# Gated linear attention and a top-1 router: attention outputs built head-columns-first in column tiles, with one scan over all head pairs

## The chip, the cores and the metric

The kernel runs on one core of a Trainium2 chip. Five engines work from queues of their own: TensorE (PE in the rows; PEld is its weight loads), VectorE (DVE), ScalarE (ACT), GpSimd (POOL) and SyncE (SP, which issues most transfers). The metric is device time in microseconds for one execution, median of the runs.

## What is computed

Attention with a gated state, then a router that sends each token to one expert of eight:

```python
batch, n_heads, seq, head_dim = (4, 8, 768, 48)
for t in range(S):
    state = alpha[:, :, t, :, None] * state + np.einsum('bhd,bhe->bhde', k[:, :, t], v[:, :, t])
    y[:, :, t] = np.einsum('bhd,bhde->bhe', q[:, :, t], state)
x = np.ascontiguousarray(attn_out.transpose(0, 2, 1, 3)).reshape(B * S, H * D)   # 3072 x 384
xn = x / (np.linalg.norm(x, axis=-1, keepdims=True) + 1e-06)
logits = xn @ en.T / tau
expert_idx = np.argmax(logits, axis=1)
...
    h = np.maximum(x[mask] @ w1[e], 0.0)
    out[mask] = gate_w[mask, None] * (h @ w2[e])
```

All is float32. A matmul that multiplies float32 leaves two records in the trace (two weight loads and two passes); a transpose leaves one.

## The kernel before

Three parts follow each other. **Attention** (lines 100 to 340) goes over 24 chunks of 128 tokens, six for each batch. **Routing** (lines 343 to 429) sorts the tokens by expert. **The expert blocks** (lines 432 to 518) gather 128 tokens at a time, run two matmuls with the expert's weights and scatter the rows. Only attention is touched by the change.

In attention the eight heads of 48 columns are padded to 64 and taken in four pairs, so that a pair fills 128 partitions after a transpose. For chunk s, `load` fetches alpha, q, k and v (`at`, `qt`, `kt`, `vt`, 192 KB each). `decays` transposes alpha, k and q on PE (`pa`, `pk`, `pq`, four transposes each), and VectorE runs two scans for each of the four pairs: `a`, the running product from the chunk's start, and `r`, the one from its end. Then `kr` = k times `r`, and `qs` = q times `a` over the chunk's whole decay. `scores` multiplies `kr` and `qs` head by head, 64 partitions at a time (`sc`), and masks them (`sm`). `update` turns `kr` back (`pkb`, copied to `kb`), multiplies it with v for the new state (`pd`) and adds the decayed old one. `rows` builds the outputs with tokens on partitions (`py`): for each pair one matmul with the decayed state and two with the masked scores. `logits` transposes those rows (`px`, copied to `xT`) and multiplies by the expert embeddings (`pl`). After the sixth chunk of a batch `choose` picks experts: a string of 13 small VectorE operations, with an activation table change on ScalarE.

The loop (lines 329 to 340) is a software pipeline: step s runs `decays(s)`, `scores` and `update` of s-1, `rows` of s-2 and `logits` of s-3. A scheduler at build time keeps nearly this order on each engine, and each engine runs its list in order. Transposed tiles share three PSUM buffers (`ps_tr`: `pa`, `pk`, `pq`, `pkb`, `px`), `pd`, `py` and `pl` three others (`ps_mm`), and `sc` has one buffer of two banks.

## Time and profile before

| | us |
|---|---|
| median of 3 runs (594.1 to 600.29) | 600.13 |
| the profiled execution | 600.23 |
| its span, first to last instruction | 598.5 |

| engine | busy, us | share of the span |
|---|---|---|
| PE | 512.8 | 86% |
| PEld | 430.7 | 72% |
| DVE | 197.9 | 33% |
| ACT | 96.1 | 16% |
| POOL | 85.1 | 14% |

Attention takes the span up to about 226 us, routing up to about 270 us, the expert blocks the rest. In the rows, a start is in microseconds from the span's first instruction. Records of PE overlap their neighbours, so that the rate of matmuls is read from the difference of two starts, not from a duration.

### The profile page before, as it was taken

What the parts mean: (1) busy time and instruction counts of PE and PEld (TensorE: products, weight loads), DVE (VectorE), ACT (ScalarE), POOL (GpSimd) and SP (SyncE); (2) the same over time, 40 slices, a digit from 0 to 9 for tenths busy, and PEclk for the clock granted to TensorE, in tenths of its full rate; (3) what the DMA queues carried; (4) which work ended last, traced back from release to release, by engine and by line L of the source; (5) the groups of instructions that cost most, each with busy time, mean ns of one, the idle gap of its engine ahead of it and who ended that gap; (6) DMA issues with size and microseconds to landing.
All of it is one profiled execution on the core that took longest, in us unless ns stands there. A gap on an engine that the chain in (4) does not pass through costs nothing.

```text
span 598.5 us, 9056 instructions
## 1 busy us (share of the span) xinstructions
PE 512.8 (86%) x3536; PEld 430.7 (72%) x3536; DVE 197.9 (33%) x602; ACT 96.1 (16%) x194; POOL 85.1 (14%) x141
## 2 busy tenths in 40 slices
PE   5799889979988993729999999999999999991993
PEld 4688778869877982618877877877877877860881
DVE  6867766784676444610001011011011011000100
ACT  2222232241232223000110100100100100100010
POOL 2110021011001000131102122122122121002010
PEclk9999999996998796558999999999999999996897
DMA  9968875673650000094084774914814939286000
GB/s 155 168 124 148 143 126 92 133 133 67 124 102 13 21 34 14 1 361 166 26 288 170 243 251 157 321 51 162 316 41 160 317 100 305 96 284 196 9 28 16
DMA packets 130011, 84.72 MB, mean 142 GB/s; under 512 B 101879, under 2 KB 121379, under 8 KB 129952
## 3 DMA queue, kind: packets, MB, share of 16 engines
q1 hardware_dynamic: 126336, 73.93, 47.2%
q0 software_dynamic: 3456, 10.03, 4.7%
q8 instruction: 31, 0.51, 0.3%
q14 instruction: 28, 0.23, 0.1%
q10 hardware_dynamic: 160, 0.01, 0.0%
HBM read 109.13 MB, written 10.03 MB: 199 GB/s over the span
## 4 chain that ended last, share of the span: by engine, by line
PE 70%; DVE 13%; issue 9%; ACT 3%; DMA 2%; another core or an unknown queue 1%; POOL 1%; POOLq 0%; ACTq 0%
PE ph L484 22%; PE pyo L494 21%; PE py L293 7%; PE py L284 4%; DVE a L202 4%; PE pd L244 4%; DVE r L203 4%; PE pl L317 3%; DMA xg<-x_rows,gidx 2%; PE pa L175 2%; PE inv L399 2%; PE sc L268 2%; DVE kr L215 2%; PE px L310 1%
## 5 line engine op out<-in xcount | busy, mean ns | idle before, releaser
L484 PEld LDWEIGHTS ph<-xgT,w 128*128 128x128 f32 x1296 | 151.4, 196 | 11.9 <-DVE xgT L477 7.9
L484 PE MATMUL ph<-xgT,w 128*128 128x128 f32 x1296 | 153.4, 279 | 5.5 <-DVE xgT L477 5.5
L494 PE MATMUL pyo<-w,hT 128*128 128x384 f32 x432 | 143.8, 486 | 0.0
L494 PEld LDWEIGHTS pyo<-w,hT 128*128 128x128 f32 x432 | 80.0, 190 | 50.1
L498 DVE TENSOR_SCALAR y<-pyo,bgate 128x384 f32<-128x384 f32 x27 | 16.7, 618 | 263.7 <-PE pyo L494 263.7
L490 ACT ACTIVATE hT<-ph 128x512 f32<-128x512 f32 x54 | 32.2, 597 | 320.9 <-PE ph L484 320.9
L293 PE MATMUL py<-vt,sm 128*128 128x48 f32 x384 | 56.4, 277 | 0.0
L499 POOL DMA_INDIRECT out_dram<-y,sidx x27 | 27.0, 1001 | 187.6 <-DVE y L498 185.2
L293 PEld LDWEIGHTS py<-vt,sm 128*128 128x128 f32 x384 | 53.0, 203 | 0.0
L202 DVE TENSOR_TENSOR_SCAN a<-pa,zeros 128x128 f32<-128x128 f32 x96 | 38.8, 404 | 22.0 <-PE pa L175 22.0
L465 POOL DMA_INDIRECT xg<-x_rows,gidx x27 | 27.9, 1032 | 105.8 <-PE pxg L475 77.9
L475 PE MATMUL pxg<-ident,xg 128*128 128x128 f32 x81 | 14.9, 320 | 27.2 <-DMA xg<-x_rows,gidx 18.6
L203 DVE TENSOR_TENSOR_SCAN r<-pa,zeros 128x127 f32<-128x127 f32 x96 | 38.0, 396 | 0.0
L284 PE MATMUL py<-decayed,qs 128*128 128x96 f32 x160 | 35.6, 306 | 0.0
L475 PEld LDWEIGHTS pxg<-ident,xg 128*128 128x128 f32 x81 | 10.9, 162 | 33.3 <-issue 30.4
L272 DVE TENSOR_TENSOR sm<-sc,causal 128x512 f32<-128x512 f32 x48 | 31.1, 678 | 1.9 <-PE sc L268 1.9
L268 PE MATMUL sc<-qs,kr 64*128 64x128 f32 x384 | 30.6, 302 | 0.0
L268 PEld LDWEIGHTS sc<-qs,kr 64*128 64x128 f32 x384 | 25.6, 203 | 4.7 <-issue 3.8
L477 DVE COPY xgT<-pxg 128x384 f32<-128x384 f32 x27 | 14.1, 550 | 42.0 <-PE pxg L475 23.5
L244 PE MATMUL pd<-vt,kb 128*128 128x96 f32 x160 | 23.3, 290 | 4.7 <-ACT kb L241 4.7
L219 DVE SCALAR_TENSOR_TENSOR qs<-pq,rend,a 128x128 f32<-128x128 f32 x96 | 26.9, 340 | 0.0
L239 PE MATMUL pkb<-ident,kr 128*128 128x128 f32 x80 | 13.5, 292 | 15.5 <-DVE r L203 15.5
(117 smaller groups left out, 391.0 us busy)
## 6 DMA issues: line engine op xcount, KB each, us to landing
w<-in_moe_w_dram SPq DMA_DIRECT2D x54, 1536.0 KB
at<-in_alpha_dram SPq DMA_DIRECT2D x24, 192.0 KB
qt<-in_q_dram SPq DMA_DIRECT2D x24, 192.0 KB
kt<-in_k_dram SPq DMA_DIRECT2D x24, 192.0 KB
vt<-in_v_dram SPq DMA_DIRECT2D x24, 192.0 KB
x_rows<-x SPq DMA_DIRECT2D x24, 192.0 KB
xg<-x_rows,gidx POOLq DMA_INDIRECT x27, 5.3
out_dram<-y,sidx POOLq DMA_INDIRECT x27, 5.8
```

Source lines behind the costliest of these rows:

```text
L202: nc.vector.tensor_tensor_scan(a[:, p], pa[:, p], zeros, 1.0, ALU.mult, ALU.add)
L203: nc.vector.tensor_tensor_scan(r[:, p, P - 2 :: -1], pa[:, p, P - 1 : 0 : -1], zeros[:, 0 : P - 1], 1.0, ALU.mult, ALU.add,)
L244: nc.tensor.matmul(pd[:, 2 * p * D : 2 * (p + 1) * D], lhsT=kb[:, p], rhs=vt[:, 2 * p : 2 * p + 2].rearrange("p h d -> p (h d)"), start=Tr ...
L268: nc.tensor.matmul(sc[:, hh, p], lhsT=kr[sl, p], rhs=qs[sl, p], start=True, stop=True)
L272: nc.vector.tensor_tensor(sm[:, hh], sc[:, hh], causal.to_broadcast([P, NP, P]), ALU.mult)
L284: nc.tensor.matmul(py[:, 2 * p * D : 2 * (p + 1) * D], lhsT=qs[:, p], rhs=decayed[:, p].rearrange("p j e -> p (j e)"), start=not opened, s ...
L293: nc.tensor.matmul(py[:, h * D : (h + 1) * D], lhsT=sm[:, hh, p], rhs=vt[:, h], start=not opened, stop=True, skip_group_check=True,)
L465: nc.gpsimd.indirect_dma_start(out=xg, out_offset=None, in_=x_rows, in_offset=bass.IndirectOffsetOnAxis(ap=gidx[:, j : j + 1], axis=0), bo ...
L484: nc.tensor.matmul(ph[:, f], lhsT=w1_t[:, i, (f0 + f) * P : (f0 + f + 1) * P], rhs=xgT[:, i], start=(i == 0), stop=(i == KT - 1),)
L490: nc.scalar.activation(hT[:, f0 : f0 + 4], ph, AF.Relu)
L494: nc.tensor.matmul(py, lhsT=hT[:, f], rhs=w2_t[:, f], start=(f == 0), stop=(f == FT - 1))
L499: ins = nc.gpsimd.indirect_dma_start(out=out, out_offset=bass.IndirectOffsetOnAxis(ap=sidx[:, j : j + 1], axis=0), in_=y, in_offset=None, ...
```

## The change

- **Outputs.** `py` now has head columns on partitions and tokens in the free dimension. `mix_states` (four matmuls of 128 x 128, with the decayed state as weights) and `mix_chunk` (eight matmuls with 64 columns of weights, each head writing its own half of the partitions: a column tile) replace the twelve matmuls of `rows`. The result is copied to `yT`.
- **Rows and logits.** Four matmuls `px`, with `yT` as weights and a constant `sel` as the moving operand (96 columns that pick the tokens' rows, 8 that are the expert embeddings), give both. They replace the three transposes `px`, the copy `xT` and three matmuls `pl`. The four logit parts are added by one VectorE reduction.
- **State.** `pd` is computed head by head in column tiles (eight matmuls, 64 weight columns and 64 moving columns) in place of four matmuls of pairs. The state is 128 x 256, and its decayed copy `dec` is block diagonal, written by two GpSimd operations on 64 partitions each; the sum is two VectorE operations.
- **Scans.** One scan of 511 and one of 512 elements replace eight of 127 and 128. They are restarted at the pair borders by a zero in alpha (a GpSimd memset of the first token's row in `at`) and a start value in the second operand (`inr`, `ini`). The lost first alpha comes from a separate small load `a0`, turned at the start into `al0`. `qs` is one operation for four.
- **Order.** Step s now begins with `keys_back(s-1)`, `mix_states(s-2)` and `rows(s-3)`, ahead of `decays(s)`; `mix_chunk(s-2)` comes last. k is loaded ahead of q.

The core of the diff:

```diff
         def load(s):
...
             nc.sync.dma_start(out=at_s[i][:, :, 0:D], in_=a_r[b, c])
+            nc.gpsimd.memset(at_s[i][0:1], 0.0)
+            nc.sync.dma_start(out=kt_s[i][:, :, 0:D], in_=k_r[b, c])
             nc.sync.dma_start(out=qt_s[i][:, :, 0:D], in_=q_r[b, c])
...
+            a0 = work.tile([NS, H, DP], FP32, name="a0", bufs=1)
+            nc.gpsimd.memset(a0[:, :, D:DP], 1.0)
+            for b in range(B):
+                nc.scalar.dma_start(
+                    out=a0[b * NCH : (b + 1) * NCH, :, 0:D], in_=a_r[b, :, 0]
+                )
...
-            for p in range(NP):
-                nc.vector.tensor_tensor_scan(a[:, p], pa[:, p], zeros, 1.0, ALU.mult, ALU.add)
-                nc.vector.tensor_tensor_scan(
-                    r[:, p, P - 2 :: -1], pa[:, p, P - 1 : 0 : -1], zeros[:, 0 : P - 1],
-                    1.0, ALU.mult, ALU.add,
-                )
+            nc.vector.tensor_tensor_scan(
+                r[:, L - 2 :: -1], pa[:, L - 1 : 0 : -1], inr[:, L - 2 :: -1],
+                1.0, ALU.mult, ALU.add,
+            )
...
+            nc.vector.tensor_tensor_scan(a, pa, ini, 0.0, ALU.mult, ALU.add)
...
+            for p in range(NP):
+                for hh in range(2):
+                    h = 2 * p + hh
+                    nc.tensor.matmul(
+                        pd[DP * hh : DP * hh + DP, p],
+                        lhsT=kb[:, h * DP : (h + 1) * DP],
+                        rhs=vt[:, h],
+                        start=True, stop=True,
+                    )
...
+        def mix_states(s):
+            d = st[s]
+            d["py"] = py = ps_mm.tile([P, NP, P], FP32, tag="mm", name="py")
+            dec = d.get("dec")
+            if dec is not None:
+                for p in range(NP):
+                    nc.tensor.matmul(
+                        py[:, p], lhsT=dec[:, p].rearrange("p j e -> p (j e)"),
+                        rhs=d["qs"][:, p],
+                        start=(p == 0), stop=False, skip_group_check=True,
+                    )
+
+        def mix_chunk(s):
+
+            d = st[s]
+            py, sm, vt = d["py"], d["sm"], vt_s[s % NBV]
+            for p in range(NP):
+                for hh in range(2):
+                    nc.tensor.matmul(
+                        py[DP * hh : DP * hh + DP, p],
+                        lhsT=vt[:, 2 * p + hh], rhs=sm[:, hh, p],
+                        start=("dec" not in d and p == 0), stop=True, skip_group_check=True,
+                    )
+            d["yT"] = yT = work.tile([P, NP, P], FP32, name="yT")
+            nc.scalar.copy(yT, py)
...
+            yT = st[s]["yT"]
+            px = ps_mm.tile([P, NP, 2 * D + E], FP32, tag="mm", name="px")
+            for p in range(NP):
+                nc.tensor.matmul(px[:, p], lhsT=yT[:, p], rhs=sel[:, p], start=True, stop=True)
+            x = work.tile([P, NP, 2 * D], FP32, name="x", bufs=3)
+            nc.scalar.copy(x, px[:, :, 0 : 2 * D])
+            nc.vector.tensor_reduce(
+                lg[:, s].unsqueeze(2), px[:, :, 2 * D :].rearrange("t p e -> t e p"),
+                axis=AX.X, op=ALU.add,
+            )
...
             if s + 2 < NS:
                 load(s + 2)
+            if 0 <= s - 1 < NS:
+                keys_back(s - 1)
+            if 0 <= s - 2 < NS:
+                mix_states(s - 2)
+            if 0 <= s - 3 < NS:
+                rows(s - 3)
             if s < NS:
                 decays(s)
             if 0 <= s - 1 < NS:
+                decay_state(s - 1)
                 scores(s - 1)
                 update(s - 1)
             if 0 <= s - 2 < NS:
-                rows(s - 2)
-            if 0 <= s - 3 < NS:
-                logits(s - 3)
+                mix_chunk(s - 2)
```

**PE, one full chunk in the second batch's pipeline.** The order's counts are matmuls as written; each that is no transpose leaves two records. Before:

```order
L175 MATMUL pa<-ident,at_124 128x128 x4
L175 MATMUL pk<-ident,kt_132 128x128 x4
L175 MATMUL pq<-ident,qt_128 128x128 x4
L268 MATMUL sc<-qs,kr 128x128 x8
L239 MATMUL pkb<-ident,kr 128x128 x4
L310 MATMUL px<-ident,x 128x128 x3
L244 MATMUL pd<-vt,kb 128x96 x4
L284 MATMUL py<-decayed,qs 128x96
L293 MATMUL py<-vt,sm 128x48 x2
```

The last two rows stand there four times, and `pl` x3 ends the step. Of the change, from the same transposes on:

```order
L216 MATMUL pa<-ident,at_118 128x128 x4
L216 MATMUL pk<-ident,kt_126 128x128 x4
L216 MATMUL pq<-ident,qt_122 128x128 x4
L326 MATMUL sc<-qs,kr 128x128 x8
L303 MATMUL pd<-vt_129,kb 64x64 x8
L352 MATMUL py<-sm,vt_128 64x128 x8
L275 MATMUL pkb<-ident,kr 128x128 x4
L340 MATMUL py<-qs,dec_168 128x128 x4
L365 MATMUL px<-sel,yT 128x104 x4
```

`pkb` has moved behind the other work of its step, `pd` and `py` work in halves of 64 columns, and `pl` is gone.

**VectorE, one chunk.** (The order calls a scan SCALAR_TENSOR_TENSOR.) Before:

```order
L202 SCALAR_TENSOR_TENSOR a<-pa,zeros 128x128
L203 SCALAR_TENSOR_TENSOR r_149<-pa,zeros 128x127
L202 SCALAR_TENSOR_TENSOR a<-pa,zeros 128x128
L203 SCALAR_TENSOR_TENSOR r_149<-pa,zeros 128x127
L202 SCALAR_TENSOR_TENSOR a<-pa,zeros 128x128
L203 SCALAR_TENSOR_TENSOR r_149<-pa,zeros 128x127
L202 SCALAR_TENSOR_TENSOR a<-pa,zeros 128x128
L203 SCALAR_TENSOR_TENSOR r_149<-pa,zeros 128x127
L209 RECIPROCAL rend<-a 128x4
L272 TENSOR_TENSOR sm<-sc,causal 128x512
L215 TENSOR_TENSOR kr<-pk,r_149 128x512
L219 SCALAR_TENSOR_TENSOR qs<-pq,rend,a 128x128 x4
```

Of the change:

```order
L368 TENSOR_REDUCE lg<-px 128x8
L246 SCALAR_TENSOR_TENSOR r_152<-pa,inr 128x511
L253 TENSOR_TENSOR kr<-pk,r_152 128x512
L256 RECIPROCAL ini_154<-r_152 128x4
L260 SCALAR_TENSOR_TENSOR a<-pa,ini_154 128x512
L266 TENSOR_TENSOR qs<-pq,a 128x512
L330 TENSOR_TENSOR sm<-sc,causal 128x512 x2
L315 TENSOR_TENSOR state<-pd,dec_166 64x256 x2
```

The logits' reduction now stands ahead of the scans of the next chunk, and `kr` comes between the two scans.

**GpSimd, the third and fourth chunk.** Of the change:

```order
L228 MEMSET at_116 1x512
L263 TENSOR_TENSOR end<-r_151,al_173 128x4
L228 MEMSET at_117 1x512
L287 TENSOR_TENSOR dec_166<-state,end 64x4x64 x2
L263 TENSOR_TENSOR end<-r_152,al_173 128x4
```

Before, `ends` and `decayed` simply took turns there. Now a memset that waits for a later chunk's alpha to land stands ahead of each decayed state.

## Rows read from the trace of the kernel before

**Rows 1.** The page's part 4: shares of the chain that ended last, by engine

```profile
PE 70%; DVE 13%; issue 9%; ACT 3%; DMA 2%; another core or an unknown queue 1%; POOL 1%; POOLq 0%; ACTq 0%
```

**Rows 2.** Stretch, length, busy PE, PEld, DVE, ACT, POOL; clock, DMA share, GB/s

```profile
6.58:52.46 45.88, 39.59 (x328) 34.79 (x328) 34.74 (x104) 8.39 (x19) 5.16 (x10) 1.00 0.97 149
52.46:104.24 51.78, 45.66 (x420) 41.19 (x420) 37.61 (x119) 14.19 (x34) 6.27 (x16) 1.00 0.74 127
104.24:159.94 55.70, 49.97 (x420) 45.89 (x420) 37.71 (x119) 15.47 (x35) 6.27 (x16) 0.91 0.57 107
159.94:225.80 65.86, 59.93 (x498) 55.27 (x498) 39.40 (x123) 17.86 (x42) 6.28 (x16) 0.90 0.23 52
```

**Rows 3.** PE in order of time, 85 to 95 us: start, us, line, records

```profile
85.30 0.51 PE L310 MATMUL px<-ident,x 128*128 128x128 f32 x3
85.64 0.60 PE L175 MATMUL pa<-ident,at 128*128 128x128 f32 x4
...
87.99 1.16 PE L268 MATMUL sc<-qs,kr 64*128 64x128 f32 x16
89.71 0.66 PE L239 MATMUL pkb<-ident,kr 128*128 128x128 f32 x4 [0.56 <-DVE r L203]
90.50 0.55 PE L310 MATMUL px<-ident,x 128*128 128x128 f32 x3
91.04 1.13 PE L244 MATMUL pd<-vt,kb 128*128 128x96 f32 x8
92.01 0.39 PE L284 MATMUL py<-decayed,qs 128*128 128x96 f32 x2
...
94.65 0.80 PE L317 MATMUL pl<-embT,xT 128*128 128x8 f32 x6
95.31 0.31 PE L175 MATMUL pa<-ident,at 128*128 128x128 f32 x1
```

**Rows 4.** PE's weight loads in the same stretch

```profile
87.99 0.97 PEld L268 LDWEIGHTS sc<-qs,kr 64*128 64x128 f32 x16 [0.17 <-issue]
91.04 0.97 PEld L244 LDWEIGHTS pd<-vt,kb 128*128 128x128 f32 x8 [0.23 <-ACT kb L241]
```

**Rows 5.** Groups of VectorE, 52 to 104 us: busy us, mean ns, idle before; L365 later

```profile
L202 DVE TENSOR_TENSOR_SCAN a<-pa,zeros 128x128 f32<-128x128 f32 x24 | 9.7, 404 | 3.6 <-PE pa L175 3.6
L272 DVE TENSOR_TENSOR sm<-sc,causal 128x512 f32<-128x512 f32 x12 | 7.7, 677 | 0.0
L215 DVE TENSOR_TENSOR kr<-pk,r 128x512 f32<-128x512 f32 x6 | 4.1, 689 | 0.1
L255 DVE TENSOR_TENSOR state<-pd,decayed 128x384 f32<-128x384 f32 x4 | 2.2, 546 | 0.0
...
L365 DVE TENSOR_TENSOR_SCAN start<-nb,zeros 128x8 f32<-128x8 f32 x1 | 0.2, 175 | 0.0
```

**Rows 6.** Groups of ScalarE and GpSimd, 52 to 104 us

```profile
L232 POOL TENSOR_TENSOR decayed<-state,ends 128x384 f32<-128x384 f32 x5 | 4.1, 828 | 16.8 <-DVE state L255 13.6 <-ACT state L253 3.3
L301 ACT COPY x<-py 128x384 f32<-128x384 f32 x7 | 3.4, 479 | 22.8 <-PE py L293 22.8
L241 ACT COPY kb<-pkb 128x512 f32<-128x512 f32 x5 | 2.9, 586 | 16.0 <-PE pkb L239 16.0
```

**Rows 7.** Busy time by stretch: two idle spots of PE and what follows each

```profile
130.00:134.00 4.00, 1.63 (x19) 1.20 (x15) 4.00 (x18) 0.83 (x2) 1.32 (x7) 1.00 0.98 177
134.00:144.00 10.00, 10.00 (x53) 9.67 (x53) 3.92 (x13) 1.47 (x4) 0.83 (x1) 0.54 0.25 59
```

**Rows 8.** The span's start in order of time, ScalarE, SyncE and PE

```profile
1.42 0.36 ACTq L127 DMA_DIRECT2D rtau<-in_moe_tau_dram  x1
4.21 0.79 SPq L183 DMA_DIRECT2D at<-in_alpha_dram  x1
6.19 0.45 PE L138 MATMUL pe<-ident,emb 8*128 8x8 f32 x3 [6.19 <-DVE emb L135]
6.58 1.11 PE L175 MATMUL pa<-ident,at 128*128 128x128 f32 x4
```

**Rows 9.** Busy time by stretch while the first chunks load

```profile
15.00:30.00 15.00, 11.49 (x109) 9.93 (x107) 12.88 (x37) 3.33 (x7) 2.07 (x4) 1.00 1.03 168
```

More of the change, by code (lines that the diff above doesn't have):

```diff
@@ L67 @@
     nc.gpsimd.memset(zeros, 0.0)
-    half = consts.tile([P, NP, 2], FP32)
-    nc.gpsimd.memset(half, 0.0)
-    nc.gpsimd.memset(half[0:DP, :, 0:1], 1.0)
-    nc.gpsimd.memset(half[DP:P, :, 1:2], 1.0)
     cols_i = consts.tile([P, P], I32)
@@ L90 @@
     rtau = consts.tile([P, 1], FP32)
-    embT = consts.tile([P, KT, E], FP32)
     gidx = consts.tile([P, NBLK], I32)
@@ L101 @@
         pads = c1.enter_context(tc.tile_pool(name="pads", bufs=1))
-        loads = c1.enter_context(tc.tile_pool(name="loads", bufs=6))
         work = c1.enter_context(tc.tile_pool(name="work", bufs=2))
@@ L111 @@
         kt_s = [pads.tile([P, H, DP], FP32, name=f"kt{i}") for i in range(NBUF)]
+        vt_s = [pads.tile([P, H, DP], FP32, name=f"vt{i}") for i in range(NBV)]
         for i in range(NBUF):
@@ L115, with prepare @@
             nc.vector.memset(kt_s[i][:, :, D:DP], 0.0)
+        for i in range(NBV):
+            nc.vector.memset(vt_s[i][:, :, D:DP], 0.0)
         NR = 3
-        r_s = [pads.tile([P, NP, P], FP32, name=f"r{i}") for i in range(NR)]
+        r_s = [pads.tile([P, NP * P], FP32, name=f"r{i}") for i in range(NR)]
+        ini_s = [pads.tile([P, NP * P], FP32, name=f"ini{i}") for i in range(2)]
+        inr = pads.tile([P, NP * P], FP32, name="inr")
+        nc.gpsimd.memset(inr, 0.0)
         for i in range(NR):
-            nc.vector.memset(r_s[i][:, :, P - 1 : P], 1.0)
+            nc.vector.memset(r_s[i][:, NP * P - 1 :], 1.0)
+        for i in range(2):
+            nc.vector.memset(ini_s[i], 0.0)
+        for p in range(NP - 1):
+            nc.gpsimd.memset(inr[:, p * P + P - 1 : (p + 1) * P], 1.0)
+        ND = 3
+        dec_s = [pads.tile([P, NP, 2, DP], FP32, name=f"dec{i}") for i in range(ND)]
+        for i in range(ND):
+            nc.gpsimd.memset(dec_s[i], 0.0)
         chunk_of = "b h (c p) d -> b c p h d"
         a_r, q_r, k_r, v_r = (t.rearrange(chunk_of, p=P) for t in (alpha, q, k, v))
-        def prepare_experts():
+        sel = pads.tile([P, NP, 2 * D + E], FP32, name="sel")
+        al0 = pads.tile([P, NP, NS], FP32, name="al0")
+        def prepare():
             emb = work.tile([E, DM], FP32, name="emb", bufs=1)
@@ L207, in decays @@
-            end = a[:, :, P - 1 : P]
-            rend = work.tile([P, NP, 1], FP32, name="rend")
-            nc.vector.reciprocal(rend, end)
-            if c > 0:
-                d["ends"] = ends = work.tile([P, NP, 2], FP32, name="ends", bufs=3)
-                nc.gpsimd.tensor_tensor(ends, half, end.to_broadcast([P, NP, 2]), ALU.mult)
+            nc.vector.tensor_tensor_scan(
+                r[:, L - 2 :: -1], pa[:, L - 1 : 0 : -1], inr[:, L - 2 :: -1],
+                1.0, ALU.mult, ALU.add,
+            )
@@ new lines, in keys_back, with decay_state @@
+        def keys_back(s):
+            if s % NCH == NCH - 1:
+                return
+            kr = st[s]["kr"]
+            pkb = ps_tr.tile([P, NP * P], FP32, tag="tr", name="pkb")
+            for p in range(NP):
+                nc.tensor.transpose(pkb[:, p * P : (p + 1) * P], kr[:, p], ident)
+            st[s]["kb"] = kb = work.tile([P, NP * P], FP32, name="kb")
+            nc.scalar.copy(kb, pkb)
+        def decay_state(s):
+            if s % NCH == 0:
+                return
+            d = st[s]
+            dec = d["dec"] = dec_s[s % ND]
+            for hh in range(2):
+                sl = slice(DP * hh, DP * hh + DP)
+                nc.gpsimd.tensor_tensor(
+                    dec[sl, :, hh], carried["state"][sl],
+                    d["end"][sl].to_broadcast([DP, NP, DP]), ALU.mult,
@@ L300, in rows @@
-            d["x"] = x = work.tile([P, DM], FP32, name="x", bufs=3)
-            nc.scalar.copy(x, py[:, 0:DM])
-            nc.sync.dma_start(out=x_rows[s * P : (s + 1) * P], in_=x)
-            x2 = work.tile([P, DM], FP32, name="x2")
-            nc.scalar.activation(x2, x, AF.Square, accum_out=sq[:, s : s + 1])
-        def logits(s):
-            x = st[s]["x"]
-            px = ps_tr.tile([P, 512], FP32, tag="tr", name="px")
-            for j in range(KT):
-                nc.tensor.transpose(
-                    px[:, j * P : (j + 1) * P], x[:, j * P : (j + 1) * P], ident
-                )
-            xT = work.tile([P, KT, P], FP32, name="xT")
-            nc.scalar.copy(xT.rearrange("p j t -> p (j t)"), px[:, 0 : KT * P])
-            pl = ps_mm.tile([P, 512], FP32, tag="mm", name="pl")
-            for j in range(KT):
-                nc.tensor.matmul(
-                    pl[:, 0:E], lhsT=xT[:, j], rhs=embT[:, j],
-                    start=(j == 0), stop=(j == KT - 1),
-                )
-            nc.vector.tensor_copy(lg[:, s], pl[:, 0:E])
+                nc.tensor.matmul(px[:, p], lhsT=yT[:, p], rhs=sel[:, p], start=True, stop=True)
```

130 lines of the change are left out of this document (60 added, 70 removed).

## The prediction

> **What bounds the kernel now.** I read the chain that ended last first: TensorE carries 70% of it and VectorE 13% [rows 1]. Then I split the span into stretches [rows 2]. The first row begins with the first alpha transpose; each of the first three ends where the next batch's begins, and the last ends with attention. In the undisturbed second batch TensorE is busy for 45.66 of 51.78 us, VectorE for 37.61, ScalarE for 14.19, and the transfers take a 0.74 share. So attention is TensorE's, with VectorE close behind. Third I read one chunk of TensorE in order of time, by differences of starts [rows 3]. Three transposes take 85.30 to 85.64, 0.11 us for each record. The eight records of `pd` (96 moving columns) take 0.97, 0.12 each. The 24 of `py` (48 and 96 columns mixed) take 92.01 to 94.65, 0.11 each, and the six of `pl` (8 columns) take 0.66, again 0.11. So up to 128 moving columns a record of the full array costs 0.11 us whatever its width. The exception is `sc`, which works in two halves of 64 rows: its 16 loads take 0.97, 0.06 each, with 0.17 us lost ahead of them [rows 4]. Two half arrays run at once.
>
> A full chunk so has 19 transposes (2.09), `sc` (0.97 + 0.17), `pd` (0.97), `py` (2.64) and `pl` (0.66), 7.50 us. A batch has six, less one `pkb` and `pd` (1.41) in the last chunk and the four state matmuls (0.88) in the first: 42.7 us. The other 9.1 of the 51.78 are waits, 1.5 a chunk. They are seen in [rows 3]: `pkb` waits 0.56 us for a buffer that the scans still read, then two hand-overs through ScalarE.
>
> **The change part by part, on TensorE.** Transposes fall from 19 to 16: 1.76. `mix_states`: 8 records of the full array, 0.88. `px`: 8 records, 0.88. `sc` stays, 1.14. `mix_chunk`: 16 records of 64 weight columns and 128 moving ones. No row shows a column tile. The nearest row is `sc`, the other way to split the array, with as many records and the same 128 columns: I take its 0.97, and 0.17 for one more change of shape. The bounds are 0.97 and 16 x 0.11 = 1.76 if halves take turns. `pd`: 16 records of 64 and 64 columns. The lower bound is half of `sc`'s 0.97, 0.49, the upper also 1.76; I take 0.73, between half and whole of the row that it is nearest to, and 0.17 for going back to the full array. Sum: 1.76 + 0.88 + 0.88 + 1.14 + 1.14 + 0.90 = 6.70 us.
>
> On the change of shape the Trainium skill (TensorEngine Tiling (Array Packing), Key Properties) says that changing the tiling mode drains TensorE. The 0.17 us ahead of `sc` agree [rows 4], and it speaks against this change, which has one such border more per chunk.
>
> **Waits of the new order.** `mix_states` of the next step needs the buffer that `yT`'s copy frees, and `px` needs `yT`. That copy is of the size of `kb`'s, 0.59 us [rows 6], and it can start only when the last record has run out, some 0.2 us behind its issue (the four of `pkb` are issued in 0.44 us and end 0.66 us after the first began [rows 3]). Only `pkb`'s 0.44 lies beside it, with its border: 0.2 us of stall, so 6.9 us a chunk. `pkb` itself has moved behind `sc`, `pd` and `py`, about 4.4 us behind its step's first transpose. The scans that held its buffer then need about 4.1 (next paragraph). That cover is thin: if VectorE is late by 1 us, about 0.7 of it shows in every chunk.
>
> **VectorE.** A scan of 128 takes 404 ns, one of 8 takes 175 [rows 5], 1.9 ns an element. So one of 512 is 404 + 384 x 1.9 = 1.14 us, against four at 404. Bounds: 1.05 (the same less the overlap of neighbours) and 1.62. Per chunk: two scans 2.28, `kr` and `qs` 0.60 each (689 ns less the overlap with the next, about 0.09), `sm` twice 1.2, the reciprocal 0.15 (a small operation: the 8-wide scan takes 0.175), the two halves of the state about 0.35 each (546 ns for 384 elements, now 256), the logits' reduction 0.2: 5.8 us. It stands now at 37.61 / 6 = 6.3. Begun 0.9 us behind the first transpose (the reduction waits for ScalarE's copy of `px`), its first scan, `kr`, reciprocal and second scan end at 0.9 + 1.14 + 0.65 + 0.2 + 1.14 = 4.1. So VectorE has about 1 us to spare in 6.9, except where `choose` adds its 13 operations of about 0.17 us, 2.2 in all: I let 1.5 us of them show per batch.
>
> **ScalarE and GpSimd.** ScalarE trades the copies `xT` for `yT`, 0.59 for 0.48, and has 14.19 of 51.78 us to do: covered. GpSimd has two multiplies on half the partitions for one of 828 ns [rows 6], at most 1.7 us, and the memset behind alpha's load. That load is issued more than one step before it is needed. The loads of one chunk are 0.786 MB, 4.7 us at the 168 GB/s of [rows 9], under 6.9. If that cover went, `dec` would come late and with it `mix_states`, at the price of the load's lateness.
>
> **The start and the end.** Four transfers for `a0` come ahead of ScalarE's first table load, about 0.4 us of issue each as for `rtau` [rows 8], 1.6 in all. GpSimd's memset for the padded embedding now stands behind the landing of the second alpha, issued at 4.21 and behind 4.7 us of the first chunk's loads, so near 8 us. The embedding's transposes, which start at 6.19, move to about 9, with four more behind them. The first alpha transpose moves from 6.58 to about 9.8: +3.2. (Bounds +2 and +5.) The last chunk's `yT` and `px` lengthen the drain by 0.6 + 0.9, and its two part steps are shorter by 0.5 each: +0.4.
>
> **Sum.** A batch: 6 x 6.9 less `pkb`, `pd` and `mix_states` once (0.44 + 0.73 + 0.88), plus 1.5: 40.9 against 51.78, a gain of 10.9. The first batch took 45.88 with the filling [rows 2]; I estimate its first three steps, which lack the later stages and go by VectorE's 4.1 us of scans, at 5.0, 5.5 and 6.0, and the rest at 3 x 6.9: 37.2, less 3.2 for the late start: gain 5.5. Batches three and four carry a stretch at the lower clock each. Where TensorE had been busy for only 1.63 of 4 us, the next 10 us ran at 0.54, that is almost wholly at 1.2 GHz in place of 2.4 [rows 7]; batch three is 3.9 longer than batch two for it [rows 2]. `choose` stays, so I leave these as they are. Gain 5.5 + 3 x 10.9 - 0.4 = 37.8. Routing and the expert blocks are untouched. The profiled execution has 600.2 (span 598.5), as has the median, 600.13: **562 us**.
>
> **Rivals.** (A) *VectorE sets the pace.* If a long scan costs four short ones (1.62) and each of five dependent operations adds 0.1 us, VectorE needs 5.8 + 1.0 + 0.5 = 7.3 us a chunk, 6 x 7.3 + 2.2 = 46.0 a batch, a gain of 5.8: 562 + 3 x 5.1 = 577. For it: VectorE is now at 73% of the batch and would be near 90%. Against: [rows 5] show the slope.
>
> (B) *Column tiles take turns.* Then the change does not do what it says. `mix_chunk` alone: +0.79 in 24 chunks, 581. `pd` too: another 1.03 in 20, 602, no change. The gain of 37.8 over 24 chunks is 1.6, so it is used up when the 32 half records cost 1.70 + 1.6 = 3.3 us, 0.10 each, which is about what a full one costs. For it: both halves of `py` write the same PSUM bank, those of `sc` write two. Against: `sc`'s halves run at once at the same width.
>
> (C) *Slower: loads stop hiding.* If in column tiles a weight load can't run beside a matmul, a record costs half a load and a full matmul, about 0.055 + 0.11 = 0.165; 32 of them are 5.3 us, +3.6 in some 22 chunks: 641. It decides from 0.10 each, as in (B). Against: eight loads and eight matmuls of `pd` fit into the same 0.97 us [rows 3, 4]. The Trainium skill (TensorE: Matmul & The Clock Gate, Part 3: Packing small matmuls — row/col tiling) would make this likelier: it has loads overlap with matmuls under way only where the row group differs, and column tiles share theirs. The trace disagrees: `pd` uses all rows in every record, and its loads are hidden all the same.
>
> **How the numbers follow.** My forecast gets 0.68, (A) 0.14, (B) 0.12, (C) 0.06. Around 562: `pd`'s bounds are 0.24 x 20 = 5 us on either side; both low-clock stretches gone would give 8, two more would cost 8; the start is worth 2. That is 549 to 577 for the likeliest case, and to take in (A) and the first half of (B) the range goes to 588. The measurement can tell about 1%, 6 us, from no change. Forecast and (A) are faster, of (B) a half is; the other half is the same, (C) slower, with a hundredth of the forecast's for a gain that something unseen takes back: faster 0.87, same 0.07, slower 0.06.
>
> **What would show it.** Right: records of `mix_chunk` in pairs, 16 in about 1 us; `pd`'s 16 in 0.5 to 1; batches of about 41 us; VectorE above 85% busy in them; the first alpha transpose near 10 us. Wrong: half records 0.11 apart (B) or more (C); TensorE waiting for VectorE ahead of `pkb` in each chunk (A); GpSimd's memset waiting long for alpha; more stretches at the low clock, since what idles TensorE there is `choose`, and that is unchanged.

## The result and the profile after

The changed kernel takes 542.65 us (median; 542.2 to 543.53) beside 600.21 for the kernel before on the same chip: ratio 0.9065, 95% interval 0.9006 to 0.9124. It is faster by 57.6 us, where 37.8 were forecast, and lies 6 us below the range: the sign and the place of the gain were right, the size was not. The profiled execution has 542.78, its span 541.0.

The chain that ended last, by engine (the page's part 4), answers to [rows 1]:

```profile
PE 58%; DVE 23%; issue 12%; DMA 2%; another core or an unknown queue 1%; POOL 1%; ACT 1%; POOLq 0%; DVEq 0%; ACTq 0%
```

VectorE carries 23% of it, up from 13. The stretches, cut as in [rows 2] (from the first alpha transpose; each to the next batch's; the last to the start of the last `x` copy), with the same columns:

```profile
10.33:45.17 34.84, 34.42 (x382) 31.12 (x382) 31.42 (x50) 8.54 (x18) 10.12 (x24) 1.00 0.86 177
45.17:82.21 37.04, 36.07 (x454) 32.97 (x453) 35.53 (x70) 14.63 (x32) 11.83 (x28) 1.00 0.82 176
82.21:120.83 38.62, 36.14 (x454) 32.96 (x453) 36.81 (x71) 15.91 (x33) 11.30 (x27) 1.00 0.71 152
120.83:168.40 47.57, 42.62 (x526) 38.47 (x524) 40.78 (x79) 19.19 (x41) 10.52 (x25) 1.00 0.29 72
```

| us | before [rows 2] | after | change | forecast |
|---|---|---|---|---|
| up to the first alpha transpose | 6.58 | 10.33 | +3.75 | +3.2 |
| batch 1 | 45.88 | 34.84 | -11.04 | -8.7 |
| batch 2 | 51.78 | 37.04 | -14.74 | -10.9 |
| batch 3 | 55.70 | 38.62 | -17.08 | -10.9 |
| batch 4, to its last `x` | 65.86 | 47.57 | -18.29 | -10.5 |
| the rest of the span | 372.7 | 372.6 | -0.1 | 0 |

All of the gain lies in the attention part. Two things stand out. TensorE's granted clock is 1.00 in all four stretches, where batches 3 and 4 had 0.91 and 0.90. And VectorE is busy for 35.53 of 37.04 us in batch 2 (96%), as near to the batch's length as TensorE with 36.07.

One chunk of TensorE in order of time (start, us, line, records), which answers to [rows 3]:

```profile
33.07 0.60 PE L216 MATMUL pa<-ident,at 128*128 128x128 f32 x4
33.50 0.60 PE L216 MATMUL pk<-ident,kt 128*128 128x128 f32 x4
33.94 0.60 PE L216 MATMUL pq<-ident,qt 128*128 128x128 f32 x4
34.47 1.16 PE L326 MATMUL sc<-qs,kr 64*128 64x128 f32 x16
35.56 0.69 PE L303 MATMUL pd<-vt,kb 128*64 128x64 f32 x16
36.08 1.05 PE L352 MATMUL py<-sm,vt 128*64 128x128 f32 x16
37.05 0.66 PE L275 MATMUL pkb<-ident,kr 128*128 128x128 f32 x4
37.55 1.06 PE L340 MATMUL py<-qs,dec 128*128 128x128 f32 x8
38.44 1.04 PE L365 MATMUL px<-sel,yT 128*128 128x104 f32 x8
39.31 0.60 PE L216 MATMUL pa<-ident,at 128*128 128x128 f32 x4
```

By differences of starts the chunk takes 39.31 - 33.07 = 6.24 us, with no wait in it. `mix_chunk` (line 352) issues its 16 records in 0.97, `pd` its 16 in 0.52. The trace has the single records too: within `sc` and `mix_chunk` two half records start together every 0.11 us, as long as one full record takes, and within `pd` every 0.06. Where the tiling changes, from `pq` to `sc`, from `sc` to `pd` and from `mix_chunk` to `pkb`, 0.20 us lie between two starts, about 0.1 more. The weight loads show these places as pauses, as in [rows 4]:

```profile
34.47 0.97 PEld L326 LDWEIGHTS sc<-qs,kr 64*128 64x128 f32 x16 [0.17 <-DVE state L315]
35.56 0.55 PEld L303 LDWEIGHTS pd<-vt,kb 128*64 128x64 f32 x16
36.02 0.86 PEld L352 LDWEIGHTS py<-sm,vt 128*64 128x64 f32 x16
37.05 0.42 PEld L275 LDWEIGHTS pkb<-ident,kr 128*128 128x128 f32 x4 [0.17 <-issue]
```

The loads pause for 0.17 us ahead of `sc`, for 0.12 ahead of `pd` (34.47 + 0.97 = 35.44) and for 0.17 ahead of `pkb`; from `pd` to `mix_chunk`, both in column tiles, they overlap. The 0.97 of `mix_chunk` holds its change back to the full array already (8 pairs at 0.11, and 0.1). `mix_states` starts 0.50 behind `pkb`: the stall of 0.2 is not there.

One of VectorE's groups in batch 2 (busy us, mean ns | idle before), which answers to [rows 5]:

```profile
L260 DVE TENSOR_TENSOR_SCAN a<-pa,ini 128x512 f32<-128x512 f32 x6 | 7.3, 1218 | 0.2
```

A long scan takes 1.22 us, forecast 1.14. The waits of batches 2 and 3 (us, times, longest):

```profile
POOL at L228 <- DMA at<-in_alpha_dram: 10.8, 8, 2.6
PE pkb L275 <- DVE kr L253: 3.2, 5, 1.1
```

TensorE waits for VectorE 5 times in 12 chunks: ahead of the first `pkb` of each batch (0.66 and 0.87), where the step before lacks the `pkb` and the `pd` of a last chunk, and three times behind the choice of the batch before (up to 1.09). Behind the third choice, in batch 4, it waits 1.44. GpSimd's memset does wait for alpha, but TensorE does not wait for it in these batches.

### The profile page after: what moved, and what is told of

Same layout as the page of the kernel before. It is cut to its first block, busy times and chain, and to the rows that moved or that the text cites. A ratio compares the mean times of both kernels' runs of the same rounds, so it can differ in the third digit from the quotient of the medians.

```text
span 541.0 us, 9273 instructions
## 1 busy us (share of the span) xinstructions
PE 465.5 (86%) x3677; PEld 388.2 (72%) x3677; DVE 195.6 (36%) x415; ACT 98.0 (18%) x190; POOL 109.8 (20%) x200
## 4 chain that ended last, share of the span: by engine, by line
PE 58%; DVE 23%; issue 12%; DMA 2%; another core or an unknown queue 1%; POOL 1%; ACT 1%; POOLq 0%; DVEq 0%; ACTq 0%
PE ph L543 25%; PE pyo L553 23%; DVE r L246 4%; DVE sm L330 4%; DVE a L260 4%; DVE kr L253 2%; PE inv L458 2%; DVE state L315 2%; PE sc L326 1%; DMA xg<-x_rows,gidx 1%; DVE qs L266 1%; PE px L365 1%; DVE xgT L536 1%; PE pkb L275 1%
## 5 line engine op out<-in xcount | busy, mean ns | idle before, releaser
L543 PEld LDWEIGHTS ph<-xgT,w 128*128 128x128 f32 x1296 | 151.6, 196 | 11.9 <-DVE xgT L536 7.9
L287 POOL TENSOR_TENSOR dec<-state,end 64x256 f32<-64x256 f32 x40 | 24.4, 609 | 68.1 <-DVE state L315 45.9
L534 PEld LDWEIGHTS pxg<-ident,xg 128*128 128x128 f32 x81 | 10.9, 162 | 33.3 <-issue 30.6
L326 PE MATMUL sc<-qs,kr 64*128 64x128 f32 x384 | 28.8, 291 | 1.7 <-DVE sm L330 1.4
L246 DVE TENSOR_TENSOR_SCAN r<-pa,inr 128x511 f32<-128x511 f32 x24 | 29.2, 1217 | 1.7 <-PE pa L216 1.2
L260 DVE TENSOR_TENSOR_SCAN a<-pa,ini 128x512 f32<-128x512 f32 x24 | 29.3, 1219 | 0.7
L326 PEld LDWEIGHTS sc<-qs,kr 64*128 64x128 f32 x384 | 24.1, 193 | 6.0 <-DVE sm L330 2.7
L365 PE MATMUL px<-sel,yT 128*128 128x104 f32 x192 | 25.3, 275 | 0.7 <-ACT yT L358 0.7
L352 PE MATMUL py<-sm,vt 128*64 128x128 f32 x384 | 25.3, 274 | 0.0
L365 PEld LDWEIGHTS px<-sel,yT 128*128 128x128 f32 x192 | 23.3, 192 | 1.2 <-ACT yT L358 0.9
L358 ACT COPY yT<-py 128x512 f32<-128x512 f32 x24 | 14.1, 586 | 53.7 <-PE py L352 53.7
L340 PE MATMUL py<-qs,dec 128*128 128x128 f32 x160 | 21.6, 278 | 0.0
```

Source lines behind the costliest of these rows:

```text
L246: nc.vector.tensor_tensor_scan(r[:, L - 2 :: -1], pa[:, L - 1 : 0 : -1], inr[:, L - 2 :: -1], 1.0, ALU.mult, ALU.add,)
L260: nc.vector.tensor_tensor_scan(a, pa, ini, 0.0, ALU.mult, ALU.add)
L326: nc.tensor.matmul(sc[:, hh, p], lhsT=kr[sl, p], rhs=qs[sl, p], start=True, stop=True)
L352: nc.tensor.matmul(py[DP * hh : DP * hh + DP, p], lhsT=vt[:, 2 * p + hh], rhs=sm[:, hh, p], start=("dec" not in d and p == 0), stop=True, ...
L365: nc.tensor.matmul(px[:, p], lhsT=yT[:, p], rhs=sel[:, p], start=True, stop=True)
L534: nc.tensor.transpose(px[:, i], xg[:, i * P : (i + 1) * P], ident)
```

## The experiments

In all of them the switch over the extra expert blocks, which runs three for this input, is replaced by three fixed blocks, in the kernel before as in the changed one. Two runs measure these bases, and all others are compared with them: 583.29 us (582.22 to 588.39) for the kernel before, 523.25 (522.75 to 524.76) for the changed one, 60.0 apart. From the first routing matmul to the end, where no other edit reaches, the profiles of these runs take 345.6 to 348.3 us. So a difference of times below that spread is read from attention's own stretches.

```diff
-        for n in tc.Switch(more, NBLK - NS + 1):
-            for j in range(NS, NS + n):
-                block(j)
+        for j in range(NS, NS + 3):
+            block(j)
```

> The kernel before, with the switch over the number of extra expert blocks replaced by the three blocks that this input needs; the base for the runs that have the same. Attention's part is unchanged, about 226 us. Also a second look at the low clock there. Theory 1 (the low-clock stretches follow TensorE's idle time at the choice of experts, by chance of timing): one to three of them, not all in the same batches as in the first profile. Rival (fixed places of the program): in batches three and four again. The three last blocks took 54 us behind the switch and 11.2 each elsewhere, so 575 to 590 us in all.

> The changed kernel with the same fixed three extra blocks. Attention as in the changed kernel, about 169 us to the end of its logits; 57 us below the kernel before with the fixed tail, 518 to 533 us.

Both came inside what was expected. The low clock of the kernel before now lies in batches 2 and 3, where it lay in 3 and 4 [rows 2]: it has no fixed place in the program.

### Where the low clock went: the order and the choice

**The order alone.** Into the kernel before only the later place of `pkb` and its copy `kb` is taken over:

```diff
+        def keys_back(s):      # the transposes pkb and the copy kb, taken out of update(s)
...
+            if 0 <= s - 1 < NS:
+                keys_back(s - 1)
             if s < NS:
                 decays(s)
```

> The kernel before (fixed tail) with one part of the change: the transposes that turn kr back (pkb) and their copy move to the start of the next step, ahead of the next alpha transposes. Theory 1 (TensorE's waits of about 1.5 us a chunk come from pkb standing behind scans that hold its buffer, and the order alone takes most of them away): undisturbed batches of 45 to 47 us in place of 51.8, 17 to 27 us below the kernel before with the fixed tail. Rival (the waits come back in another place, and only fewer and cheaper records gain): batches of 50 to 52 us, within 6 us of it.

549.79 us (548.95 to 550.99): 33.5 of the 60.0, with every matmul of the kernel before, and more than the 17 to 27 expected, which counted no low clock. Its batch 2, columns as in [rows 2], ahead of it the base's batches 2 and 3:

```profile
52.68:110.83 58.15, 52.73 (x421) 48.19 (x420) 37.82 (x119) 14.29 (x34) 6.28 (x16) 0.85 0.66 113
110.83:168.98 58.15, 52.73 (x421) 48.21 (x420) 37.82 (x119) 15.56 (x35) 6.28 (x16) 0.85 0.54 103
48.60:94.81 46.21, 45.55 (x421) 41.81 (x420) 37.11 (x119) 12.74 (x34) 6.17 (x16) 1.00 0.85 147
```

An undisturbed batch falls from 51.78 [rows 2] to 46.21: TensorE hardly waits any more, but for a short pause in each chunk (below). The four batches give 4.1, 11.9, 12.0 and 5.2. The two large ones hold 58.15 - 51.78 = 6.4 us of low clock each, and that is gone too.

**The choice at the end.** In the kernel before, all four calls of `choose` stand behind the last chunk:

```diff
-            if s % NCH == NCH - 1:
-                choose(s // NCH)
+            if s == NS - 1:
+                for b in range(B):
+                    choose(b)
```

> The kernel before (fixed tail) with the choice of experts for all four batches behind the last chunk, so that its VectorE operations hold nobody up between batches. Theory 1 (the low-clock stretches follow TensorE's idle time of about 2 us at the choice): none in attention, which saves what they cost (12.7 us in the profile of the kernel before with the fixed tail); each batch 1 us shorter; the end 6 to 9 us longer: 572 to 580 us. Rival (idle time at the choice is not the cause): one to three stretches as before, 583 to 592 us.

568.07 us (567.84 to 568.32), 15.2 less than its base and 4 below the lower bound of theory 1; no low clock is left in attention. Batches 2 and 3 take 50.43 each at full clock. So in the kernel before it is `choose`, met by a `pkb` that waits for VectorE, that brings the low clock: without it 12.7 of the 15.2 us are regained at once. The base shows how (PE in order of time, behind the first choice and behind the third; then stretches of 4 us behind the first):

```profile
77.74 1.16 PE L268 MATMUL sc<-qs,kr 64*128 64x128 f32 x16
80.59 0.90 PE L239 MATMUL pkb<-ident,kr 128*128 128x128 f32 x4 [1.69 <-DVE r L203]
...
196.89 0.66 PE L239 MATMUL pkb<-ident,kr 128*128 128x128 f32 x4 [1.70 <-DVE r L203]
```

```profile
78.00:82.00 4.00, 1.80 (x20) 1.21 (x18) 4.00 (x18) 0.98 (x3) 1.32 (x7) 0.86 1.18 195
82.00:86.00 4.00, 3.83 (x18) 3.83 (x19) 2.22 (x7) 0.12 (x1) 0.83 (x1) 0.50 0.49 53
...
94.00:98.00 4.00, 3.96 (x26) 3.34 (x25) 3.44 (x10) 1.06 (x2) 0.20 (x1) 0.51 0.57 98
98.00:102.00 4.00, 4.00 (x38) 4.00 (x38) 0.56 (x1) 0.54 (x2) 0.83 (x1) 1.00 0.01 2
```

TensorE is busy for 1.80 of 4 us around the choice, and then works at 1.2 GHz up to about 98 us. The wait alone does not decide it. TensorE stands for 1.69 to 1.70 us behind each of the first three choices, in this base and in the kernel before alike; the low clock follows four of the six times, and in this base not behind the third. Batch 4, which so ran at full clock here, is 5.5 us shorter than the 65.86 of [rows 2]:

```profile
168.98:229.37 60.39, 54.03 (x498) 49.09 (x498) 39.25 (x123) 17.84 (x42) 6.28 (x16) 1.00 0.25 57
```

**The idle time put back into the changed kernel.** Useless VectorE operations hang on the choice of the first three batches, first six of them, then two:

```diff
+            if b < B - 1:
+                lag = work.tile([P, NP * P], FP32, name="lag")
+                nc.vector.tensor_scalar(lag, inr, best[:, 0:1], None, ALU.mult)
+                for _ in range(5):      # the second run: once
+                    nc.vector.tensor_tensor_scan(lag, lag, inr, 0.0, ALU.mult, ALU.add)
```

> The changed kernel (fixed tail) with six useless VectorE operations of 512 elements (about 7 us) tied to the choice of experts in each of the first three batches. Theory 1 (several us without work let TensorE's clock fall, and its next 10 to 17 us run at 1.2 GHz): at least two of the three places show a stretch at the lower clock, each for 4 to 6 us beyond the 5 to 7 us of waiting; 549 to 565 us. Rival (the clock in the changed kernel stays up for another reason): only the waiting, 537 to 545 us.

> Base: the changed kernel with the fixed tail, 523.25 us. Two useless VectorE operations of 512 (about 0.65 and 1.22 us, as kr and the scan in its rows) hang on the end of the choice of the first three batches, against six in the run before (which cost 17.0 us and brought one low-clock stretch behind each choice, of 3.4 to 6.8 us). Theory 1: what matters is how long TensorE stands behind the choice; it now stands about 1.1 us there in the worst case and the clock stays full, with 1.9 us more it stands 2 to 3 us, which is what the kernel before had (up to 1.7 us at a time), and at least one of the three choices is followed by a low clock: 3 x 1.9 = 5.7 us and 1.7 to 3.4 more for each stretch, 531 to 538. Rival: so short an idle time alone does not bring it; what the kernel before had was idle time again and again (17 waits of 0.5 to 1.7 us ahead of pkb in two batches), not one pause: all at full clock, 527 to 529.

With six: 540.27 us (539.47 to 540.91), +17.0, and a low-clock stretch behind each of the three choices. With two: 528.97 (528.44 to 530.43), +5.7. Both times are what the rival gave, yet the low clock came, as theory 1 had it: with two operations it follows the first two choices (waits of 2.29 and 2.71 us) and not the third (2.70). The stretches are only short. TensorE with six, then with two, then the stretches with two:

```profile
72.46 1.12 PE L280 MATMUL pkb<-ident,kr 128*128 128x128 f32 x4 [5.53 <-DVE kr L258]
```

```profile
70.01 0.89 PE L279 MATMUL pkb<-ident,kr 128*128 128x128 f32 x4 [2.29 <-DVE kr L257]
```

```profile
64.00:68.00 4.00, 3.71 (x59) 3.18 (x57) 3.87 (x14) 1.47 (x5) 2.67 (x5) 1.00 0.62 142
68.00:72.00 4.00, 1.99 (x11) 1.99 (x12) 3.94 (x8) 0.93 (x2) 1.44 (x6) 0.79 0.53 107
72.00:76.00 4.00, 4.00 (x35) 3.83 (x36) 3.19 (x6) 1.10 (x3) 1.22 (x2) 0.79 0.14 43
```

So the low clock can come back in the changed kernel when TensorE stands longer behind the choice. In the changed kernel the new place of `pkb` leaves at most 1.45 us of idle time there, where the kernel before had 1.69, and no low clock followed. What decides between two equal waits stays open.

### What the column tiles are worth

First `mix_chunk` alone, then `pd` too, is issued with all first halves ahead of all second halves, so that neighbouring records use the same column tile:

```diff
-            for p in range(NP):
-                for hh in range(2):
+            for hh in range(2):
+                for p in range(NP):
                     nc.tensor.matmul(
```

> The changed kernel (fixed tail) with mix_chunk's loops swapped, so that the four matmuls of one 64-column half come before the four of the other, and neighbours share a column tile. Theory 1 (the column tiles run two at a time, and that is where TensorE gains): 16 records at 0.11 in place of 0.06, 0.98 becomes about 1.76, +0.78 in each of 24 chunks, +19 us on the changed kernel with the fixed tail. Rival (the gain is VectorE's and the order's, TensorE has time to spare): +1 to +7 us.

> Base: the changed kernel with the fixed tail, 523.25 us. Both sets of column-tile matmuls (mix_chunk and the state's pd) are written with all first halves ahead of all second halves, so that no two records of different column tiles stand next to each other. mix_chunk alone in this order took 1.46 us for its 16 records instead of 0.97 and cost 4.5 us of time. Theory 1: pd goes from 0.51 to about 0.9 (16 x 0.06 to 0.09 us is 0.9 to 1.46), a chunk to 7.1 to 7.7 us, which is longer than VectorE's work per chunk (6.0), so all of it now shows: 20 x 0.4 to 0.95 more than the run with one of them, 536 to 547. Rival: pd's records have 64 columns to load and 64 to send, and what bounds them is something else than the pairing: pd stays at 0.5 to 0.6 and the time within 2 us of 527.75.

527.75 us (526.82 to 528.0), +4.5, and 529.39 (528.78 to 530.38), +6.1: both times are what the rivals gave. `mix_chunk` alone in turn:

```profile
68.58 0.69 PE L303 MATMUL pd<-vt,kb 128*64 128x64 f32 x16
69.09 1.53 PE L352 MATMUL py<-sm,vt 128*64 128x128 f32 x16
70.56 0.66 PE L275 MATMUL pkb<-ident,kr 128*128 128x128 f32 x4
```

Its 16 records take 1.47 instead of 0.97. One by one, five of the same half in a row start 0.11 us apart, as full records do; only six in the middle, where the end of the first half meets the start of the second, still run in pairs. With `pd` in turn as well, the two together take 2.09 instead of 1.48. Batch 2 of the base and of the run with both:

```profile
44.43:81.91 37.48, 36.15 (x455) 32.97 (x454) 35.98 (x71) 14.62 (x32) 11.86 (x28) 1.00 0.81 173
46.62:85.94 39.32, 39.32 (x455) 36.45 (x454) 36.16 (x71) 14.64 (x32) 11.90 (x28) 1.00 0.76 162
```

TensorE's work grows by 3.17 us, the batch by 1.84. The other 1.33 us were idle time in the base, in which TensorE waited for VectorE. So running side by side is real, but taking most of it away costs no more than 6 of the 60 us here.

### VectorE as the next bound

**Eight short scans instead of two long ones:**

```diff
-            nc.vector.tensor_tensor_scan(a, pa, ini, 0.0, ALU.mult, ALU.add)
+            for p in range(NP):
+                sl = slice(p * P, (p + 1) * P)
+                nc.vector.tensor_tensor_scan(a[:, sl], pa[:, sl], ini[:, sl], 0.0, ALU.mult, ALU.add)
```

(and `r` likewise)

> The changed kernel (fixed tail) with each long scan cut into its four pairs again, eight scans of 127 and 128, all else as in the change. Theory 1 (long scans bring VectorE nothing: the two take 1.31 and 1.33 from start to next start, eight short ones 8 x 0.316 = 2.53): -1 to +3 us. Rival (long scans save VectorE 0.9 us a chunk, and VectorE is the bound): +0.9 x 24, +22 us.

523.66 us (522.98 to 524.98): no difference to be measured, as theory 1 had it. The one scan for all head pairs brings nothing by itself.

**Half of the mask moved, then left out:**

```diff
-            for hh in range(2):
-                nc.vector.tensor_tensor(
-                    sm[:, hh], sc[:, hh], causal.to_broadcast([P, NP, P]), ALU.mult
-                )
+            nc.vector.tensor_tensor(
+                sm[:, 0], sc[:, 0], causal.to_broadcast([P, NP, P]), ALU.mult
+            )
+            nc.scalar.copy(raw, sc[:, 1])       # the second run: neither of these two, sm[:, 0] for both
+            nc.gpsimd.tensor_tensor(
+                sm[:, 1], raw, causal.to_broadcast([P, NP, P]), ALU.mult
+            )
```

> Base: the changed kernel with the fixed tail, 523.25 us. Half of the causal masking of the scores (one of VectorE's two sm operations of about 0.65 us per chunk) goes by a copy on ScalarE and a multiplication on GpSimd. Theory 1: VectorE, busy for 36.0 to 36.8 us of batches that take 37.5 to 38.6, shares the bound with TensorE (36.1); with 6 x 0.65 = 3.9 us less per batch only TensorE's 36.1 is left, and the batches fall to 36.1 to 36.6: 3 to 5 us less, 518 to 520.5. Rival: the second half of sm comes later by the copy and the multiplication (0.6 and about 0.8 us), mix_chunk or pkb waits for it, or GpSimd, which also sets alpha's row and the state's decay, becomes late for the next chunk: no gain or a loss, 523 to 533.

> Base: the changed kernel with the fixed tail, 523.25 us. The causal masking of the second heads is left out of the computation, and the masked scores of the first heads stand in for it: the same matmuls, and one VectorE operation of 512 less per chunk (about 0.65 us), with no work added elsewhere (the run before moved it to ScalarE and GpSimd, and the copy stood ahead of yT's on ScalarE, so it told nothing on VectorE's share). Theory 1: in the four batches TensorE is busy for 36.1 us of 37.5 to 38.6, and what is left are waits for VectorE; without 6 x 0.65 us of VectorE's work per batch these shrink to what the choice costs: batches of 36.2 to 37, the attention 4 to 7 us shorter, 516 to 519.5. Rival: the waits are those of the choice and of single hand-overs (kr, the state, sm), not VectorE's rate: batches as before to 0.4 us, 521.5 to 523.

Both missed, on the slow side: 556.25 us (554.4 to 557.27), +33.0, and 533.62 (533.48 to 534.11), +10.4. In the first the copy `raw` waits for VectorE, `yT`'s copy stands behind it on ScalarE, and TensorE's `px` waits for `yT`; five low-clock stretches of 3.4 us follow such waits and are part of the loss (the waits from 60 to 130 us):

```profile
ACT raw L333 <- DVE sm L329: 32.7, 8, 4.8
PE px L369 <- ACT yT L362: 12.4, 8, 2.3
```

In the second, which adds no work, VectorE gets ahead and waits in turn (in order of time):

```profile
83.06 1.04 PE L364 MATMUL px<-sel,yT 128*128 128x104 f32 x8
84.14 0.48 ACT L366 COPY x<-px 128x384 f32<-128x384 f32 x1 [1.18 <-PE px L364]
84.65 0.19 DVE L367 TENSOR_REDUCE lg<-px 128x8 f32<-128x32 f32 x1 [2.07 <-ACT x L366]
84.87 1.22 DVE L246 TENSOR_TENSOR_SCAN r<-pa,inr 128x511 f32<-128x511 f32 x1
...
89.54 0.86 DVE L315 TENSOR_TENSOR state<-pd,dec 64x256 f32<-64x256 f32 x2
...
90.56 1.11 PE L364 MATMUL px<-sel,yT 128*128 128x104 f32 x8 [1.47 <-DVE state L315]
```

The reduction `lg` stands ahead of the next scan and waits for ScalarE's `x`; the scans, the masks and the state follow; and the next `px` waits for that state. From `px` to `px` this ring takes 90.56 - 83.06 = 7.50 us, longer than the 6.24 of the changed kernel's chunk. It does not hold everywhere: the loss lies in the first two batches (39.37 and 41.56 for 33.79 and 37.48), the third loses 1.0 and the fourth gains 0.6, and the first chunk of a batch takes 5.78 for 6.92, without its wait for VectorE ahead of `pkb`. So neither run tells what VectorE's rate alone is worth in the whole. That stays with the 1.33 us a batch above and the 96% of its busy time; a faster version with less VectorE work was not found.

### The late start

Three versions move the preparation of the experts' table. The first writes `prepare()` behind `decays(0)`. The second also loads the table on SyncE's queue and prepares behind the third chunk's decays, with the first-alpha transposes alone behind `decays(0)`. The third is the first with the scaling of the table on ScalarE:

```diff
-        prepare()
         for s in range(NS + 3):
...
+            if s == 0:
+                prepare()
...
-            nc.vector.tensor_scalar(
-                embp[:, :, 0:D], emb.rearrange("e (h d) -> e h d", d=D), en, None, ALU.mult
-            )
+            nc.scalar.activation(       # the third version
+                embp[:, :, 0:D], emb.rearrange("e (h d) -> e h d", d=D), AF.Copy, scale=en
+            )
```

> The changed kernel (fixed tail) with prepare() called behind the first chunk's decays, so that TensorE's transposes of the embeddings and of a0 no longer stand ahead of the first alpha transpose. The first alpha transpose moves from 10.7 to about 7 us, the kernel gains 3 to 4 us, about 519.5 us, if nothing else holds the start. Rival (the first chunks are held by transfers or VectorE anyway): within 1 us.

> Base: the changed kernel with the fixed tail, 523.25 us, whose first alpha transpose runs at 10.3 us. The preparation of the experts' table is written behind the decays of the third chunk with its loads on SyncE's queue, and the small first-alpha transposes behind those of the first chunk, so that the first scan stands ahead of the preparation on VectorE (in the earlier try it stood behind it, ran at 9.20, and nothing was gained). Theory 1: the first alpha transpose runs at about 5.7 and the first scan at about 7 instead of about 11.5, and the 3.5 to 4.5 us reach the end: 518.5 to 520. Rival: the loads of chunks 2 and 3, which the queues deliver at their own pace (the 16 DMA engines are busy for 0.89 of the first batch), or the preparation inside the third chunk take the gain back: 522 to 525.

> Base: the changed kernel with the fixed tail, 523.25 us. The preparation stands behind the decays of the first chunk as in the run of 522.45 us, where the first scan waited at 9.20 us behind VectorE's scaling of the experts' table, which waits for GpSimd's memset; the scaling now goes by ScalarE, which is idle then. Theory 1: the first scan runs at about 7.9, the second alpha transpose at 12.0 to 12.6 instead of 13.8, no preparation stands in the third chunk (as in the run of 521.55 us), and 2.5 to 4 us reach the end: 519 to 520.8. Rival: the first batch is held by the landing of the loads or by the chunk's own 6.25 us, and what is gained at the start is given back in the first batch: 521.3 to 523.

522.45 us (521.73 to 522.59), 521.55 (521.25 to 522.54) and 520.36 (520.12 to 520.49): the first is what its rival gave, the second lies between theory 1 and rival, the third is theory 1. At the first routing matmul the first two are only 0.9 us ahead of the base. In the first the first scan still ran at 9.20, behind the scaling. In the second it ran at 7.20, but the preparation in the third chunk gave most of that back: the fourth chunk's first alpha transpose came at 28.12, in the base at 25.93. The third starts so:

```profile
5.75 1.11 PE L216 MATMUL pa<-ident,at 128*128 128x128 f32 x4 [5.75 <-POOL at L228]
7.89 1.20 DVE L246 TENSOR_TENSOR_SCAN r<-pa,inr 128x511 f32<-128x511 f32 x1
11.91 0.94 PE L216 MATMUL pa<-ident,at 128*128 128x128 f32 x4
```

Against its base the first alpha transpose is 4.9 us earlier (5.75 for 10.64), the second batch 2.7 (41.74 for 44.43), the first routing matmul 3.55 (171.26 for 174.81), the time 2.9. So the late start does reach the end of attention, for the most part, as the sum had it. This version is the fastest of all: 0.6% less than its base.

## Why the prediction was right or wrong, step by step

**Right.** TensorE is the bound and attention the place. The waits ahead of `pkb` go with the new order. The column tiles run in pairs, 16 records of `mix_chunk` in 0.97, as taken. The scan is 1.22 us in bounds of 1.05 to 1.62. VectorE is busy above 85%. The first alpha transpose is at 10.33 (about 9.8 forecast), with GpSimd's memset of the padded table at 8.17. The transfers stay hidden. (B) and (C) did not come.

**Wrong: "`choose` stays, so I leave these as they are".** This step carries 9.4 of the 19.7 us missed: 3.9 in batch 3, as the prediction read it itself, and 5.5 in batch 4 (65.86 against the 60.39 of the same batch in the base, at full clock). The sum had nothing for the two stretches going; the range had 8 us for it, and the signs of being wrong named more low clock, not less. It took the choice for the cause. The low clock follows TensorE's idle time, which in the kernel before is the choice's work and a `pkb` that waits for VectorE. Of these only the first stays. The prediction had itself moved `pkb` 4.4 us behind its step's first transpose and did not carry that cover over to the choice. The runs with the order alone, with the choice at the end and with idle time put back show it from three sides.

**Wrong in size: 6.9 us a chunk.** It is 6.24 to 6.25. `pd` was 0.73 + 0.17 and is 0.52; `mix_chunk` was 0.97 + 0.17 and is 0.97; the stall behind `yT`, 0.2, is nothing; all else is 0.09 longer. The range took in `pd`'s bounds alone: the two allowances and the stall, 0.54 a chunk together, had none at zero, so it could not hold them. In batch 2 the chunks give 6 x 0.65 = 3.9 us, all of its excess of 3.86; in three batches that excess is 11.6. The allowance of 0.17 for a change of tiling was not wrong as a price, it was counted twice: the 0.97 of [rows 4] runs to the end of `sc`'s last load, while 8 pairs of half records start within 0.88, so 0.97 had room for a change of 0.1. Nor does `pd` go back to the full array: `mix_chunk` follows it in the same tiling. The rule of the Trainium skill (TensorEngine Tiling (Array Packing), Key Properties), that a change of the tiling mode drains TensorE, spoke for the allowance. The trace agrees: 0.20 us lie between two starts where the tiling changes, 0.11 within `sc` and `mix_chunk`.

**The rest.** The first batch was 2.3 us better than its estimate, batches 3 and 4 wait about 1.6 longer each than batch 2, and the start was 0.55 later: 9.4 + 11.6 + 2.3 - 3.2 - 0.55 = 19.55, of 19.7.

**Two errors that cancelled in part: the split of the gain.** I counted 9.1 us of waits in a batch and 42.7 of issue, and let the order take 7.6 of the waits (all but 1.5 for the choice). [rows 2] have TensorE idle for 6.1, and the order alone took away 5.6. In that run a full chunk still takes 7.94 us, where I had 7.50; most of the difference is a pause of 0.33 ahead of `pl`, which waits for `xT`. The busy time hides half of it, since a record lasts longer than the 0.11 to the next start:

```profile
86.86 0.60 PE L230 MATMUL pkb<-ident,kr 128*128 128x128 f32 x4
87.63 0.83 PE L323 MATMUL pl<-embT,xT 128*128 128x8 f32 x6 [0.17 <-ACT xT L320]
```

The matmuls, with `pl` and its pause gone, gave 46.21 - 37.04 = 9.2 where I had 42.7 - 39.4 = 3.3.

**(A) is half true.** VectorE does not set the pace at 577, but it takes 1.3 us of a batch from TensorE, and with 35.53 and 36.07 us busy in a batch the two engines are about even. That fewer matmuls alone would now gain little is what I expect from this; no run shows it.

## What to carry to other kernels

A stretch at the lower clock follows idle time of TensorE, not the operations that stand there: when a change moves a wait, forecast the stretch again, as a chance. Before calling the rest of a stretch waits, list the pauses between starts one by one, since short ones don't show in the busy time. Look whether a measured row holds an allowance already before adding it, and give every small allowance (a change of tiling, a stall) zero as its lower bound. Work taken from the busier engine can start a ring of waits elsewhere; look at what stands next on each queue first.
